# Second product of the second feed-forward: 512-wide accumulation replaced by seven 256-wide Strassen products for three of four block pairs

## Chip, cores and metric

The kernel runs on one core of a Trainium2 chip. The metric is device microseconds of one execution. The engines are called as in the profile: PE (TensorE matmuls), PEld (its weight loads), DVE (VectorE), ACT (ScalarE), POOL (GpSimd) and SP (the queue that issues almost all DMAs). A difference of less than 0.2% (3 us) can hardly be told from no change here.

## What is computed

A cross attention of 8 batches (512 tokens and 32 states each, 8 heads of 64) gives 4352 rows of 512 values: 8 blocks of 512 tokens and one block of 256 state rows. They pass through two feed-forward layers; the second one is what the change touches:

```python
def _moe_ref(x, w_gate, w_val, w_out) -> np.ndarray:
    gate = 1.0 / (1.0 + np.exp(-(x @ w_gate)))
    val = x @ w_val
    return (gate * val @ w_out).astype(np.float32)

def _moe2_ref(x, w_in, w_out) -> np.ndarray:
    h = x @ w_in
    r = np.maximum(h, 0.0)
    g = r * r
    return (g @ w_out).astype(np.float32)
```

`w_in` is 512 x 2048 and `w_out` 2048 x 512. All matmuls take every operand as a high and a low part (`h`, `l`), so one product of two tiles is three matmuls (`mm3`, lines 182 to 184 before).

## The kernel before

The program has a first part (attention, weight conversion, first feed-forward, up to about 795 us) and a second part, the second feed-forward. Python code emits instructions; a scheduler then sets each engine's order, so that work of neighbouring steps is interleaved on PE. The second part goes over the 8 token blocks in `NP` = 4 pairs `p`. A pair has `NQ` = 8 steps `q`, each for 256 of the 2048 hidden columns.

`front(p, q)` forms the hidden values of both blocks by Strassen's method: seven products P1 to P7 of sums of x blocks (made once for each pair by `x_steps`, split into `xh`, `xl` by `split_x`) with sums of `w_in` blocks (`wi`, made in the first part). A product is 6 matmuls of 512 columns, so a front has 42. The PSUM tiles are `px`, `py`, `pz`; ACT copies intermediate sums out (`snap`), DVE joins them (`joined`), and `squared` applies relu and square and splits the result `c` into `g2h`, `g2l`.

`back(p, b, r, nt)` is the second product, called after q = 2, 4, 6, 7 with r = 0 to 3: for one block `b` and four 128-row pieces of `w_out` (`wo[f]`) it accumulates, for each 128-token tile, 12 matmuls of 512 columns into a PSUM tile `o`; the result goes to `y2` by an ACT copy (r = 0) or a DVE add (r > 0), and out by DMA after r = 3. `load_wo(r)` loads four `wo` tiles of 512 KB. At the end of a pair, with `apart`, the matmuls on the older pieces come first and `x_steps(p + 1)` is emitted around `back`.

In pair 0, `load_late` and `convert_late` still convert the second half of `w_out` and store it in DRAM; POOL's only work in the second part is their subtraction `ul` (line 661). In the last pair the 256 state rows go along: `state_front` (24 matmuls of 256 columns for each q, PSUM tile `pst`) and `back(p, 2, ...)`.

Of the kernel before, what the change touches and what calls it, by code (L numbers as in the profile page):

```python
# [8 lines left out]
F32 = mybir.dt.float32  # L9
# [9 lines left out]
P = 128  # L19
# [13 lines left out]
def kernel(  # L33
# [127 lines left out]
    def width(b):  # L161
        return S if b < B else NSTATE
# [13 lines left out]
    NQ = NF2 // 2  # L176
    wi_dram = {q: dram.tile([P, 8, 2, 256], F32, name=f"wi{q}") for q in range(NQ)}
    wo_dram = {f: dram.tile([P, 2, 512], F32, name=f"wo{f}") for f in range(NF2)}
    y_dram = {b: dram.tile([P, KD, width(b)], F32, name=f"yd{b}") for b in blocks}

    def mm3(ps, lh, ll, rh, rl, start, stop, more=False):
# [550 lines left out]

    def close_one():
        one.close()
        for name, bufs in (("wo", 4), ("g2", 24), ("y2", 8), ("t2", 1)):
# [27 lines left out]
        wi_done[1] += 1  # L763
        return wi.pop(key)

    def load_wo(r):
        for f in range(4 * r, 4 * r + 4):
            t = two["wo"].tile([P, 2, 512], F32R, tag="wo", name="wo")
            nc.sync.dma_start(out=t.bitcast(F32), in_=wo_dram[f])
            wo[f] = t  # L770

    def load_xin(p, i):
        half, b = ((0, 0), (0, 1), (1, 1), (1, 0))[i]
# [11 lines left out]
    def x_steps(p):  # L785

        t1, t2 = {}, {}

        def one_two(k):
            b11, b12, b22 = (xin[p, i, j][:, k, :] for i, j in ((0, 0), (0, 1), (1, 1)))  # L790
            split_x(p, "P1", k, b11)
            t1[k] = cv_p.tile([P, S], F32, tag="c", name="t1")
            nc.vector.tensor_sub(out=t1[k], in0=b12, in1=b11)
            split_x(p, "P5", k, t1[k])
            t2[k] = q_p.tile([P, S], F32, tag="q", name="t2")
            nc.vector.tensor_sub(out=t2[k], in0=b22, in1=t1.pop(k))
# [27 lines left out]
    def snap(ps, name):  # L824
        t = two["t2"].tile([P, S], F32, tag=name, name=name)
        nc.scalar.copy(out=t, in_=ps)  # L826
        return t
# [14 lines left out]
        nc.vector.tensor_sub(out=l, in0=c, in1=h.bitcast(F32))  # L842
        g2[key] = (h, l)

    def front(p, q):
# [16 lines left out]
        squared((p, 0, 2 * q), joined(y, p1))
        product(x, p, q, "P7", False)
        c22 = joined(x, p5)
        product(z, p, q, "P3", False)
        squared((p, 1, 2 * q + 1), c22)
        product(x, p, q, "P4", False)
        squared((p, 1, 2 * q), joined(z, u))
        squared((p, 0, 2 * q + 1), x, raw=True)

    def back(p, b, r, nt, apart=False):
        fs = range(4 * r, 4 * r + 4)
        accs2 = [acc_p.tile([P, S], F32, tag=f"acc{t}", name=f"o{t}") for t in range(nt)]
        order = [(t, f) for t in range(nt) for f in fs]
        if apart:
            order.sort(key=lambda k: k[1] // 2)
        for t, f in order:
            ts = slice(t * P, (t + 1) * P)
            gh, gl = g2[p, b, f]
            mm3(  # L880
                accs2[t], gh[:, ts], gl[:, ts], wo[f][:, 0, :], wo[f][:, 1, :],
                f == fs[0], f == fs[-1],
            )
            if f < fs[-1]:
                continue
            acc = accs2[t]
            if r == 0:
                y = (two["y2"] if b < 2 else yo_p).tile([P, DM], F32, tag="y2" if b < 2 else "y", name="y2")
                y2[b, t] = y
                nc.scalar.copy(out=y, in_=acc)  # L890
                continue
            y = y2[b, t]
            nc.vector.tensor_add(out=y, in0=acc, in1=y)  # L893
            if r < NQ // 2 - 1:
                continue
            if b == 2:
                for i in range(4):
                    r0 = (4 * t + i) * (S + NS) + S
                    (nc.scalar if i % 2 else nc.sync).dma_start(
                        out=out[r0 : r0 + NS, :], in_=y[NS * i : NS * (i + 1), :]  # L900
                    )
            else:
                r0 = (2 * p + b) * (S + NS) + t * P
                nc.sync.dma_start(out=out[r0 : r0 + P, :], in_=y)

    def prep_state_x():
        t = two["t2"].tile([P, KD, NSTATE], F32, tag="xst", name="xst")
        nc.sync.dma_start(out=t, in_=y_dram[B])
        for k in range(2):
            h = gs_p.tile([P, 2, NSTATE], F32R, tag="gh", name="sth")  # L910
            l = gs_p.tile([P, 2, NSTATE], F32R, tag="gl", name="stl")
# [3 lines left out]
            xop["s", k] = (h, l)  # L915

    def state_front(p, q):
# [10 lines left out]
        hl = raw_p.tile([P, 2, 2 * NSTATE], F32R, tag="raw", name="g2s")  # L928
        squared("s", ps.rearrange("p i n -> p (i n)"), raw=True, into=(hl[:, 0], hl[:, 1]))
        h, l = g2.pop("s")  # L930
        for i in range(2):
            cols = slice(i * NSTATE, (i + 1) * NSTATE)
            g2[p, 2, 2 * q + i] = (h[:, cols], l[:, cols])

    HALF = NF1 // 2
    segments = [(b, 0, HALF) for b in range(QB)] + [(b, HALF, NF1) for b in range(QB)]
# [105 lines left out]

    step = lambda: None
    close_one()
    load_wo(0)
    for fn in x_steps(0):
        fn()
    last = NP - 1
    for p in range(NP):
        for q in range(NQ):  # L1050
            if p == 0 and q > 2:
                convert_late()
            if p == 0 and q == 2:
                load_late(EARLY)
            front(p, q)
            if p == last and q == 0:
                prep_state_x()
            if p == last:
                state_front(p, q)
            if p < last and NQ - 5 < q < NQ - 1:  # L1060
                load_xin(p + 1, q - NQ + 4)
            if q < 2 or q % 2 and q < NQ - 1:
                continue
            steps = []
            if q == NQ - 1:
                steps = x_steps(p + 1) if p < last else []
                for fn in steps[:3]:
                    fn()
            r = (q - 1) // 2
            for b in range(2):  # L1070
                back(p, b, r, NT, apart=q == NQ - 1)
                if p == 0:
                    convert_late()
                for fn in [] if b else steps[3:]:
                    fn()
            if p == last:
                back(p, 2, r, NSTATE // P)
            if (p, r) != (last, NQ // 2 - 1):
                load_wo((r + 1) % (NQ // 2))


# [28 lines left out]
```

## Time and profile before

| | us |
|---|---|
| median of 3 runs (1497.92 to 1499.72) | 1499.65 |
| the profiled execution, its own time | 1500.54 |
| its span, first to last instruction | 1498.8 |
| PE busy in the span | 1431.0 (95%) |
| DVE busy | 940.2 (63%) |
| ACT busy | 748.8 (50%) |
| POOL busy | 246.0 (16%) |

The profile is of one execution; 1.7 us of its own time lie outside the span. A matmul's busy time is longer than its share of the engine, since matmuls are pipelined: how fast PE works is read from the distance between the starts of neighbouring matmuls. Some matmul records are missing from the trace.

### The profile page before, as it was taken

To read this page: it belongs to the slowest core of one execution; us is meant where nothing else is said; L and a number is where in the kernel's file an instruction comes from. 1 tells how busy PE (TensorE), PEld (TensorE's weight loads), DVE (VectorE), ACT (ScalarE), POOL (GpSimd) and SP (SyncE) were. 2 spreads that over 40 slices of the span, in tenths; PEclk is the share of its full clock that TensorE was granted. 3 is DMA by queue.
4 is the path that set the end of the run, shared out by engine and by line. 5 is a ranking of instruction groups with operands and counts; after the bars stand their busy time and mean duration, and the time that the engine had idled before them with its cause. 6 is when DMAs were issued, how large, how long until landed. Compare 5 with 4: busy or idle time off the path is not lost.

```text
span 1498.8 us, 19379 instructions
## 1 busy us (share of the span) xinstructions
PE 1431.0 (95%) x6552; PEld 1176.9 (79%) x6552; DVE 940.2 (63%) x1579; ACT 748.8 (50%) x1291; POOL 246.0 (16%) x216
## 2 busy tenths in 40 slices
PE   5879999999999989999899999999999999999998
PEld 3558878887787677888798788888888888888887
DVE  7986887578889987555536655734575356433443
ACT  6865876456678887666424522332242223232211
POOL 1112213232344544333101100000000000000000
PEclk9889999999999999999999999999999999999999
DMA  9984799699999864333677844644365443645442
GB/s 265 341 263 120 229 328 339 210 363 292 323 296 286 254 211 145 95 113 92 242 271 250 274 158 147 217 146 143 133 227 188 151 152 134 222 124 195 155 145 80
DMA packets 244595, 311.68 MB, mean 208 GB/s; under 512 B 105361, under 2 KB 152977, under 8 KB 244497
## 3 DMA queue, kind: packets, MB, share of 16 engines
q1 hardware_dynamic: 242224, 309.66, 63.8%
q10 hardware_dynamic: 2272, 0.79, 0.3%
q8 instruction: 52, 0.85, 0.2%
q14 instruction: 47, 0.38, 0.1%
HBM read 221.25 MB, written 89.13 MB: 207 GB/s over the span
## 4 chain that ended last, share of the span: by engine, by line
PE 72%; DVE 10%; ACT 7%; DMA 7%; issue 3%; SPq 1%; POOL 0%; ACTq 0%; DVEq 0%; POOLq 0%
PE o L182 8%; PE o L183 8%; PE o L184 8%; PE px L183 4%; PE px L182 4%; PE px L184 4%; PE acc L183 4%; PE acc L184 3%; PE acc L182 3%; DMA raw<-in_moe_w_out_dram 2%; PE psg L182 2%; PE psg L183 2%; PE psg L184 2%; PE psv L182 2%; PE psv L183 2%
## 5 line engine op out<-in xcount | busy, mean ns | idle before, releaser
L182 PE MATMUL o<-wo,g2h 128*128 128x512 f32 x512 | 198.6, 390 | 3.7 <-DMA wo<-wo 3.0
L183 PE MATMUL o<-wo,g2h 128*128 128x512 f32 x512 | 199.1, 389 | 0.0
L184 PE MATMUL o<-wo,g2l 128*128 128x512 f32 x512 | 193.9, 389 | 0.0
L537 POOL TENSOR_TENSOR gg<-gi,gg 128x512 fp32r<-128x512 f32 x96 | 135.3, 1412 | 350.5 <-ACT gg L536 284.2
L183 PE MATMUL acc<-gl,o 128*128 128x512 f32 (+1 forms) x432 | 164.4, 381 | 3.7 <-DVE gl L190 3.7
L184 PE MATMUL acc<-gh,o 128*128 128x512 f32 (+1 forms) x432 | 163.0, 378 | 0.0
L841 ACT CAST g2h<-c 128x512 fp32r<-128x512 f32 x96 | 59.3, 622 | 178.8 <-DVE c L837 178.8
L182 PE MATMUL acc<-gh,o 128*128 128x512 f32 (+1 forms) x432 | 139.3, 380 | 0.6 <-DVE y L624 0.4
L893 DVE TENSOR_TENSOR y<-o,y 128x512 f32<-128x512 f32 x102 | 68.5, 688 | 103.5 <-PE o L184 102.8
L182 PEld LDWEIGHTS o<-wo,g2h 128*128 128x128 f32 x512 | 96.1, 188 | 24.9 <-ACT p L826 3.0
L184 PEld LDWEIGHTS o<-wo,g2l 128*128 128x128 f32 x512 | 96.1, 188 | 19.8
L183 PEld LDWEIGHTS o<-wo,g2h 128*128 128x128 f32 x512 | 96.2, 188 | 19.5
L190 DVE TENSOR_TENSOR gl<-g,gh 128x512 fp32r<-128x512 f32 (+1 forms) x108 | 88.4, 818 | 36.3 <-ACT gh L189 35.8
L182 PE MATMUL px<-xh,wi 128*128 128x512 f32 x256 | 99.8, 390 | 0.0
L183 PE MATMUL px<-xl,wi 128*128 128x512 f32 x256 | 99.7, 389 | 0.0
L184 PE MATMUL px<-xh,wi 128*128 128x512 f32 x256 | 99.6, 389 | 0.0
L183 PEld LDWEIGHTS acc<-gl,o 128*128 128x128 f32 x432 | 81.3, 188 | 21.3 <-DVE gl L190 6.9
L182 PEld LDWEIGHTS acc<-gh,o 128*128 128x128 f32 x432 | 80.6, 189 | 17.4 <-DVE y L624 1.1
L184 PEld LDWEIGHTS acc<-gh,o 128*128 128x128 f32 x432 | 81.3, 188 | 14.6
L182 PE MATMUL psg<-a,gg 128*128 128x512 f32 x192 | 78.6, 409 | 14.8 <-ACT sg L550 12.1
L556 DVE TENSOR_TENSOR g<-psv,sg 128x512 f32<-128x512 f32 x96 | 65.6, 683 | 35.4 <-PE psv L184 21.6
L189 ACT CAST gh<-g 128x512 fp32r<-128x512 f32 (+1 forms) x108 | 64.3, 596 | 40.4 <-DVE g L556 23.0
(188 smaller groups left out, 3268.7 us busy)
## 6 DMA issues: line engine op xcount, KB each, us to landing
wi<-wi SPq DMA_DIRECT2D x256, 256.0 KB, 3.1
wo<-wo SPq DMA_DIRECT2D x64, 512.0 KB, 5.5
gd<-go SPq DMA_DIRECT2D x192, 128.0 KB, 4.4
gi<-gd SPq DMA_DIRECT2D x96, 256.0 KB, 4.0
wi<-wa SPq DMA_DIRECT2D x32, 512.0 KB, 5.0
wd<-w SPq DMA_DIRECT2D x24, 512.0 KB, 5.1
ws<-wd SPq DMA_DIRECT2D x24, 512.0 KB, 6.7
raw<-in_moe_w_out_dram SPq DMA_DIRECT2D x20, 512.0 KB, 6.2
```

The source lines that it names most:

```text
L182: nc.tensor.matmul(ps, lh, rh, start=start, stop=False, skip_group_check=more)
L183: nc.tensor.matmul(ps, lh, rl, start=False, stop=False, skip_group_check=more)
L184: nc.tensor.matmul(ps, ll, rh, start=False, stop=stop, skip_group_check=more)
L189: nc.scalar.copy(out=gh[:, :n], in_=g32[:, :n])
L190: nc.vector.tensor_sub(out=gl[:, :n], in0=g32[:, :n], in1=gh[:, :n].bitcast(F32))
L537: nc.gpsimd.tensor_sub(out=t[:, 1], in0=src, in1=t[:, 0].bitcast(F32))
L556: nc.vector.tensor_mul(out=g32, in0=ps, in1=sg)
L841: nc.scalar.copy(out=h, in_=c)
L893: nc.vector.tensor_add(out=y, in0=acc, in1=y)
```

## The change

For pairs 1 to 3 the second product also goes by Strassen's method. The hidden values of a pair for one q are four 512-token blocks `c` (block b, hidden half i). `g_steps` makes sums of them on POOL (`s1`, `s2` and one in place), and splits all seven operands on ACT and DVE into `gh`, `gl`. `back_pairs` runs seven products for each r: a product has 24 matmuls of 256 columns (8 output tiles of 128 tokens by 256 columns, two q, three each), 168 for each r, where the two calls of `back` had 96 of 512 columns. Its weights are halves of `wo`, or sums of `w_out` blocks, that lie in DRAM as `wt`; a tile `wp` is two DMAs of 256 KB, four tiles ahead (`feed_wo`). The PSUM tiles are of 2 x 256 columns; after every product both are added to, or copied to, a half of `y2`: 14 evacuations for each r, where there were 8.

The weight sums are made in pair 0: `add_wo` (POOL, for each q two adds of 512 columns and four of 256) and `split_wo` (ACT cast, DVE subtraction, four DMAs of 256 KB). Pair 0's own second product stays as it was. `x_steps` emits the operands product by product and takes its subtractions to POOL for pairs 2 and 3. In the last pair `state_back(q)` does the state rows for each q, with as many matmuls as before. The core of the diff:

```diff
+    BACK = [
+        ("P1", "x", 0, 0), ("P5", "z", 1, 1), ("P6", "x", 0, 1), ("P3", "z", 0, 1),
+        ("P7", "x", 1, 1), ("P2", "y", 0, 0), ("P4", "x", 1, 0),
+    ]
...
+    def feed_wo():
+        while wo_done[0] < min(wo_done[1] + 4, len(wo_plan)):
...
+            else:
+                t = two["wo"].tile([P, 2, 2, 256], F32R, tag="wo", name="wp")
+                p, r, k = key
+                for i in range(2):
+                    q = 2 * r + i
+                    n, e = (PLAIN if k in PLAIN else SUMS)[k]
+                    w = wo_dram[2 * q + n] if k in PLAIN else wt_dram[q][:, :, n, :]
+                    nc.sync.dma_start(
+                        out=t[:, i].bitcast(F32), in_=w[:, :, 256 * e : 256 * (e + 1)]
+                    )
...
+    def add_wo(q):
+        c = []
+        for f in (2 * q, 2 * q + 1):
+            t = gs_p.tile([P, 2, 256], F32, tag="gh", name="wc")
+            w = wo[0, f].bitcast(F32)
+            nc.gpsimd.tensor_add(
+                out=t.rearrange("p e x -> p (e x)"), in0=w[:, 0, :], in1=w[:, 1, :]
+            )
+            c.append(t)
+        b1, b2 = c
+        nc.gpsimd.tensor_sub(out=b1[:, 0], in0=b1[:, 1], in1=b1[:, 0])
+        nc.gpsimd.tensor_sub(out=b1[:, 1], in0=b2[:, 1], in1=b1[:, 1])
+        nc.gpsimd.tensor_sub(out=b2[:, 1], in0=b2[:, 1], in1=b1[:, 0])
+        nc.gpsimd.tensor_sub(out=b2[:, 0], in0=b2[:, 0], in1=b2[:, 1])
+        sums[q] = c
...
+        sub = (nc.gpsimd if p > 1 else nc.vector).tensor_sub
...
+    def g_steps(p, q):
+
+        def split(name, src):
+            pool, tag = (yo_p, "y") if name == "P4" else (two["g2"], "g2")
+            h, l = [pool.tile([P, S], F32R, tag=tag, name=n) for n in ("gh", "gl")]
+            nc.scalar.copy(out=h, in_=src)
+            nc.vector.tensor_sub(out=l, in0=src, in1=h.bitcast(F32))
+            gop[p, q, name] = (h, l)
...
+        def p1():
+            v["s1"] = cv_p.tile([P, S], F32, tag="c", name="s1")
+            nc.gpsimd.tensor_add(out=v["s1"], in0=c(1, 0), in1=c(1, 1))
+            split("P1", c(0, 0))
+
+        def p5():
+            v["s2"] = q_p.tile([P, S], F32, tag="q", name="s2")
+            nc.gpsimd.tensor_sub(out=v["s2"], in0=v["s1"], in1=c(0, 0))
+            split("P5", v["s1"])
...
+    def back_pairs(p, r, extra, apart=False, between=None):
...
+            for j, t, k in order:
+                h, l = gop[p, 2 * r + k, name]
+                ts = slice((2 * j + t) * P, (2 * j + t + 1) * P)
+                mm3(
+                    ps[to, j][:, t], h[:, ts], l[:, ts], w[:, k, 0], w[:, k, 1],
+                    start and t == k == 0, k == 1, not (start and t == 0),
+                )
+            drop_wo((p, r, name))
+            for j in range(2):
...
+                y = y2[b, j][:, :, 256 * e : 256 * (e + 1)]
+                if r == 0 and name in ("P1", "P5", "P6", "P4"):
+                    nc.scalar.copy(out=y, in_=ps[to, j])
+                else:
+                    nc.vector.tensor_add(out=y, in0=ps[to, j], in1=y)
...
+            if q == NQ - 1:
+                rest_of(extra)
+                steps = x_steps(p + 1) if p < last else []
+                between = (lambda: state_back(NQ - 1)) if p == last else None
+                back_pairs(p, NR - 1, steps, apart=True, between=between)
+                rest_of(steps)
+            elif q and q % 2 == 0:
+                back_pairs(p, q // 2 - 1, extra)
+                rest_of(extra)
```

The order of instructions up to the end of the first part stays as it was. Three places show what moves after it.

DVE at the end of a pair, before (pair 1 to pair 2): four evacuations `y`, then the low parts `xl` of the next pair's operands and the subtractions `t` that two of them need.

```order
L893 TENSOR_TENSOR y_10140<-o_10746,y_10140 128x512 [waits PE_49]
L893 TENSOR_TENSOR y_10154<-o_10747,y_10154 128x512 [waits PE_49]
L893 TENSOR_TENSOR y_10168<-o_10748,y_10168 128x512 [waits PE_49]
L893 TENSOR_TENSOR y_10182<-o_10749,y_10182 128x512 [waits PE_49]
L782 TENSOR_TENSOR xl<-xin,xh 128x512 [waits PE_49,Activation_49]
L782 TENSOR_TENSOR xl<-t_10907,xh 128x512 [waits PE_49,Activation_49]
L803 TENSOR_TENSOR t_11001<-xin 128x512 [waits DVE_49]
L782 TENSOR_TENSOR xl<-t_10913,xh 128x512 [waits PE_49,Activation_49]
```

DVE at the same place now: evacuations alternate with `gl` (operands of this pair's second product) and `xl` (of the next pair's first).

```order
L1051 TENSOR_TENSOR y_10281<-o,y_10281 128x2x256 [waits PE_49]
L1051 TENSOR_TENSOR y_10283<-o,y_10283 128x2x256 [waits PE_49]
L852 TENSOR_TENSOR xl<-t,xh 128x512 [waits Activation_49]
L991 TENSOR_TENSOR gl<-s_11450,gh 128x512 [waits Activation_49]
L991 TENSOR_TENSOR gl<-c,gh 128x512 [waits Activation_49] x2
L1051 TENSOR_TENSOR y_10281<-o,y_10281 128x2x256 [waits DVE_49,PE_49]
L1051 TENSOR_TENSOR y_10283<-o,y_10283 128x2x256 [waits DVE_49,PE_49]
L852 TENSOR_TENSOR xl<-t,xh 128x512 [waits Activation_49]
L1051 TENSOR_TENSOR y_10320<-o,y_10320 128x2x256 [waits PE_49]
L852 TENSOR_TENSOR xl<-xin,xh 128x512 [waits DMAHW3_49,Activation_49]
```

From the first of the 14 evacuations of this r to the join of the next front's `px` there are 36 instructions on DVE: 14 evacuations and 2 joins (one input in PSUM) and 20 others (two inputs in SBUF).

PE, first front of the next pair, before: product P7 into `px` waits for its weights and for ACT, for no low part from DVE, and tiles `o` stand around it.

```order
L182 MATMUL px<-xh,wi 128x512 [waits DMAHW1_49,Activation_49]
L183 MATMUL px<-xl,wi 128x512
L184 MATMUL px<-xh,wi 128x512
```

PE at the same place now: P2, P7 and P3 follow one another, and each low part `xl` is waited for by itself.

```order
L184 MATMUL py<-xl,wi 128x512 [waits DVE_49]
L185 MATMUL py<-xh,wi 128x512
L183 MATMUL px<-xh,wi 128x512 [waits DMAHW2_49,Activation_49]
L184 MATMUL px<-xl,wi 128x512 [waits DVE_49]
L185 MATMUL px<-xh,wi 128x512
L183 MATMUL px<-xh,wi 128x512
L184 MATMUL px<-xl,wi 128x512 [waits DVE_49]
L185 MATMUL px<-xh,wi 128x512
L183 MATMUL pz<-xh,wi 128x512 [waits DMAHW3_49]
L184 MATMUL pz<-xl,wi 128x512 [waits DVE_49]
```

POOL, which ended before with eight `ul` of pair 0, now has, at the end of pair 1, the sums `s` and the in-place sum `c` of the last q among the subtractions `t` of `x_steps(2)`.

```order
L1001 TENSOR_TENSOR s_11444<-c 128x512
L865 TENSOR_TENSOR t<-xin 128x512
L1006 TENSOR_TENSOR s_11450<-s_11444,c 128x512
L1010 TENSOR_TENSOR c<-c 128x512
L865 TENSOR_TENSOR t<-xin,t 128x512
L865 TENSOR_TENSOR t<-xin 128x512
L1014 TENSOR_TENSOR s_11450<-c,s_11450 128x512
L865 TENSOR_TENSOR t<-xin 128x512
```

Twelve POOL instructions stand in this chain, and ACT casts and DVE's `gl` and `xl` wait for them one by one.

## Rows read from the trace of the kernel before

**Rows 1.** Windows, the four pairs: window, length, busy (count) by engine, PEclk, DMA share, GB/s

```profile
797.00:957.00 160.00, 156.96 (x696) 129.36 (x695) 104.63 (x166) 65.08 (x114) 11.46 (x8) 1.00 0.63 218
957.00:1120.00 163.00, 163.00 (x721) 134.97 (x720) 86.29 (x135) 50.03 (x86) 0.00 (x0) 1.00 0.50 168
1120.00:1284.00 164.00, 164.00 (x732) 136.06 (x732) 86.67 (x135) 49.55 (x85) 0.00 (x0) 1.00 0.47 161
1284.00:1495.00 211.00, 210.04 (x1006) 176.14 (x1004) 87.29 (x135) 50.06 (x86) 0.00 (x0) 1.00 0.45 152
```

**Rows 2.** Waits of PE, 797 to 1499 us: us in total, times, longest

```profile
PE o L182 <- DMA wo<-wo: 3.0, 2, 2.6
PE o L182 <- ACT g2h L841: 0.5, 1, 0.5
```

**Rows 3.** Timeline of PE: the first and last of 21 matmuls of 512 columns

```profile
1483.64 0.39 PE L182 MATMUL o<-wo,g2h 128*128 128x512 f32 x1
...
1488.17 0.39 PE L184 MATMUL o<-wo,g2l 128*128 128x512 f32 x1
```

**Rows 4.** Timeline of PE: the first and last of 52 matmuls of 256 columns

```profile
769.83 0.28 PE L183 MATMUL acc<-gl,o 128*128 128x256 f32 x1
...
775.95 0.28 PE L183 MATMUL psg<-sp,ws 128*128 128x256 f32 x1
```

**Rows 5.** Groups of DVE, 957 to 1284 us: busy, mean ns, idle before

```profile
L893 DVE TENSOR_TENSOR y<-o,y 128x512 f32<-128x512 f32 x52 | 34.5, 687 | 48.0 <-PE o L184 47.9
L842 DVE TENSOR_TENSOR g2l<-c,g2h 128x512 fp32r<-128x512 f32 x48 | 32.6, 688 | 11.7 <-ACT g2h L841 10.8
```

**Rows 6.** Groups of ACT, 957 to 1284 us

```profile
L841 ACT CAST g2h<-c 128x512 fp32r<-128x512 f32 x48 | 29.8, 622 | 78.7 <-DVE c L837 78.7
```

**Rows 7.** Groups of DVE, 300 to 600 us

```profile
L190 DVE TENSOR_TENSOR gl<-g,gh 128x512 fp32r<-128x512 f32 x42 | 36.3, 864 | 9.8 <-ACT gh L189 9.6
L556 DVE TENSOR_TENSOR g<-psv,sg 128x512 f32<-128x512 f32 x42 | 28.6, 680 | 7.8 <-ACT sg L550 6.4 <-PE psv L184 1.0
```

**Rows 8.** Groups of POOL, 300 to 600 us

```profile
L537 POOL TENSOR_TENSOR gg<-gi,gg 128x512 fp32r<-128x512 f32 x42 | 62.5, 1490 | 123.3 <-ACT gg L536 91.0 <-issue 22.5 <-DMA gd<-go 4.1
L690 POOL TENSOR_TENSOR c<-c 128x256 f32<-128x256 f32 x7 | 6.4, 912 | 11.4 <-DVE wa L698 8.3 <-DVE xs_t L428 3.1
```

**Rows 9.** Windows of the first part, columns as in Rows 1

```profile
300.00:400.00 100.00, 96.81 (x423) 78.58 (x422) 80.45 (x126) 62.33 (x102) 31.59 (x29) 1.00 0.98 331
400.00:500.00 100.00, 96.42 (x431) 77.73 (x430) 87.91 (x153) 81.58 (x136) 48.42 (x43) 0.98 0.96 286
500.00:600.00 100.00, 89.85 (x392) 69.76 (x392) 81.42 (x147) 80.26 (x137) 44.21 (x35) 0.98 0.64 197
600.00:700.00 100.00, 100.00 (x479) 83.68 (x478) 56.56 (x107) 67.01 (x118) 37.20 (x29) 1.00 0.36 99
```

**Rows 10.** Waits of PE, 300 to 600 us

```profile
PE psg L182 <- ACT sg L550: 7.5, 9, 3.0
PE acc L183 <- DVE gl L190: 3.5, 5, 1.6
PE psv L182 <- DVE g L556: 1.5, 5, 0.4
PE ps_so L420 <- DVE sw L411: 1.4, 1, 1.4
...
PE ps_s L183 <- DVE xtl L308: 0.8, 1, 0.8
```

**Rows 11.** Windows within pair 0, columns as in Rows 1

```profile
797.00:820.00 23.00, 22.59 (x105) 18.39 (x104) 18.73 (x30) 12.95 (x23) 2.78 (x2) 1.00 0.97 341
840.00:860.00 20.00, 17.37 (x77) 14.08 (x76) 12.81 (x20) 9.86 (x17) 4.63 (x4) 1.00 0.97 346
```

**Rows 12.** DMA issues, 797 to 1499 us: count, KB each, median us to landing

```profile
wi<-wi SPq DMA_DIRECT2D x245, 256.0 KB, 3.1
wo<-wo SPq DMA_DIRECT2D x64, 512.0 KB, 5.5
```

More of the change, by code (lines that the diff above doesn't have):

```diff
@@ L178 @@
     wo_dram = {f: dram.tile([P, 2, 512], F32, name=f"wo{f}") for f in range(NF2)}
+    wt_dram = {q: dram.tile([P, 2, 2, 512], F32, name=f"wt{q}") for q in range(NQ)}
     y_dram = {b: dram.tile([P, KD, width(b)], F32, name=f"yd{b}") for b in blocks}
@@ L764, in take_wi @@
         return wi.pop(key)
[L766 to L770, printed above, removed]
+    BACK = [
+        ("P1", "x", 0, 0), ("P5", "z", 1, 1), ("P6", "x", 0, 1), ("P3", "z", 0, 1),
+        ("P7", "x", 1, 1), ("P2", "y", 0, 0), ("P4", "x", 1, 0),
+    ]
+    NR = NQ // 2
+    wo_plan = [(0, f) for f in range(NF2)]
+    for p in range(1, NP):
+        for r in range(NR):
+            own = [(p, r, k) for k, _, _, _ in BACK]
+            if p < NP - 1:
+                wo_plan += own
+                continue
+            side = [(p, f) for f in range(4 * r, 4 * r + 4)]
+            if r < NR - 1:
+                wo_plan += side + own
+            else:
+                wo_plan += side[:2] + own[:3] + side[2:] + own[3:]
@@ new lines, in split_wo @@
+    def split_wo(q):
+        for i, c in enumerate(sums.pop(q)):
+            c = c.rearrange("p e x -> p (e x)")
+            h = gs_p.tile([P, 512], F32R, tag="gl", name="th")
+            nc.scalar.copy(out=h, in_=c)
+            nc.sync.dma_start(out=wt_dram[q][:, 0, i, :], in_=h.bitcast(F32))
+            l = gs_p.tile([P, 512], F32R, tag="gl", name="tl")
+            nc.vector.tensor_sub(out=l, in0=c, in1=h.bitcast(F32))
+            nc.sync.dma_start(out=wt_dram[q][:, 1, i, :], in_=l.bitcast(F32))
@@ L872, in back @@
+    def back(b, r, apart=False):
         fs = range(4 * r, 4 * r + 4)
[L873 to L874 removed]
+        accs2 = [acc_p.tile([P, S], F32, tag=f"acc{t}", name=f"o{t}") for t in range(NT)]
+        order = [(t, f) for t in range(NT) for f in fs]
         if apart:
@@ L1044 @@
     close_one()
-    load_wo(0)
-    for fn in x_steps(0):
-        fn()
+    feed_wo()
     last = NP - 1
-    for p in range(NP):
-        for q in range(NQ):
[L1051 to L1057, printed above, removed]
+    rest_of(x_steps(0))
+    for q in range(NQ):
+        if q > 2:
+            convert_late()
+        if q == 2:
+            load_late(EARLY)
+        front(0, q, [])
+        if NQ - 5 < q < NQ - 1:
+            load_xin(1, q - NQ + 4)
+        if q < 2 or q % 2 and q < NQ - 1:
+            continue
+        r = (q - 1) // 2
+        steps = x_steps(1) if q == NQ - 1 else []
+        for fn in steps[:7]:
+            fn()
+        add_wo(2 * r)
+        back(0, r, apart=q == NQ - 1)
+        convert_late()
+        rest_of(steps[7:])
+        split_wo(2 * r)
+        add_wo(2 * r + 1)
+        back(1, r, apart=q == NQ - 1)
+        convert_late()
+        split_wo(2 * r + 1)
+        drop_wo(*[(0, f) for f in range(4 * r, 4 * r + 4)])
+    y2.clear()
+    for p in range(1, NP):
+        extra = []
+        for q in range(NQ):
+            front(p, q, extra)
+            extra = g_steps(p, q)
             if p == last:
+                if q == 0:
+                    prep_state_x()
+                else:
+                    state_back(q - 1)
                 state_front(p, q)
```

231 lines of the change are left out of this document (161 added, 70 removed).

## Prediction

> **What bounds the kernel now.** I first read the windows over the four pairs [rows 1], the second column being PE's busy time: PE is busy for nearly the whole length of each (163.00 of 163.00, 164.00 of 164.00), at a granted clock of 1.00 (2.4 GHz). DVE is busy for about 53% of the two middle pairs, ACT for 31%, POOL not at all. Then the waits of PE over the second part: 3.5 us in 702, of which 3.0 are for `wo` [rows 2]. So the second part is PE's issue of matmuls and nothing else, and its length is a count of matmuls times the distance between two starts. For 512 columns that distance is (1488.17 - 1483.64) / 20 = 0.2265 us [rows 3]. For 256 columns, with another weight tile for each matmul, it is (775.95 - 769.83) / 51 = 0.1200 us [rows 4], not half but 53%. The check: 8 fronts of 42 and 4 backs of 96 are 336 + 384 = 720 matmuls, times 0.2265 is 163.1 us, which is the length of a middle pair.
>
> **Matmuls removed and added.** A pair's second product was 384 x 0.2265 = 87.0 us. By Strassen's method it is 4 x 168 = 672 matmuls of 256 columns, 672 x 0.1200 = 80.6 us: seven eighths of the columns, but more starts, so 7.3% is saved and not 12.5%. That is 6.34 us for a pair, 156.7 instead of 163.1, and 19.0 us for pairs 1 to 3. The state rows keep their matmuls. Everything else is a question of whether PE still never waits.
>
> **DVE in pairs 1 and 2.** A pair now has 174 DVE instructions of 128 x 512 values: 72 with an input in PSUM (24 joins, 48 additions to `y2`) and 102 with both inputs in SBUF (24 squares, 8 products of relu, 56 `gl`, 14 `xl`). Without work on POOL either kind takes 0.688 us [rows 5] (I take the 2 x 256 shape of the new evacuations as 512 columns), so 119.7 us, 76% of 156.7. ACT casts about 110 tiles at 0.62 us [rows 6], 44%: free. But POOL now works in these pairs, and between 300 and 600 us, where it works too, a DVE instruction with two SBUF inputs took 864 ns, one from PSUM 680 [rows 7]. POOL's 32 sums and 8 subtractions are 40 x 1.490 [rows 8] = 59.6 us, 38% of the pair; in that stretch it was busy for 31.59 + 48.42 + 44.21 us [rows 9], 41%, so its price is the nearest. With it, 72 x 0.688 + 102 x 0.864 = 137.6 us, 88%. That is below the length of the pair, so DVE doesn't become the bound; this needs a mean of (156.7 - 49.5) / 102 = 1.05 us, above any of these rows.
>
> A busy share of 88% without a wait isn't likely, though. The nearest stretch is the same 300 to 600 us, with DVE at 80 to 88% and POOL at 32 to 48%, where PE was busy for 90 to 97% [rows 9]. PE's waits on DVE there were 3.5 + 1.5 + 1.4 + 0.8 = 7.2 us [rows 10], 2.4% (the 7.5 us for `sg` are an ACT result that the second part doesn't have). At 600 to 700 us, with DVE at 57%, there was none [rows 9]. I take 2.4% of 2 x 156.7 us, that is 7.5 us; the ends are 0 and twice that.
>
> Where they would lie: the PSUM pair of a product must be evacuated (2 x 0.688 us) before the product two later needs it, while a product gives PE 24 x 0.120 = 2.88 us, so DVE keeps up with about two splits for each product. The tight place is the end of a pair, where the last sums of `g`, the subtractions of the next pair's x and the 14 evacuations meet. From the first of these evacuations to the join of the next `px` DVE has 36 instructions, 16 x 0.688 + 20 x 0.864 = 28.3 us, and PE has about 28.8 us of work in the same stretch (seven products of 2.88 and six groups of six matmuls, 36 x 0.2265, with 0.5 to spare). So about 3 us of waits at each of these two places is already within the 7.5. Behind a late `gl` on DVE stands the next evacuation, and behind that the next product on PE.
>
> **Pair 3.** 192 DVE instructions (86 from PSUM) at the same prices are 86 x 0.688 + 106 x 0.864 = 150.8 us in about 201 us, 75%, with state matmuls to fill in; no next pair follows. Between 0 and 2.4% of 201, that is 0 and 4.8: I take 1.5. The last work is now the state rows of the last step, after the evacuation of the last product: 0.3 us.
>
> **Pair 0.** `add_wo` gives POOL 16 additions of 512 columns and 32 of 256, 16 x 1.490 + 32 x 0.912 [rows 8] = 53.0 us; `split_wo` gives DVE 16 subtractions, which add at least 16 x 0.864 = 13.8 us to its 104.6 [rows 1], 74%, and at most, with every instruction dearer by 0.864 / 0.688, come to 145 us, 91%. The 32 writes of 256 KB are 8.4 MB, 52 GB/s over 160 us on top of 218 [rows 1]. The mean has room, but at 797 to 820 and 840 to 860 us the DMA engines were already at a share of 0.97, with 341 and 346 GB/s [rows 11], and PE waited 3.0 us for `wo` there [rows 2]. Below, the cost is 0 (the writes fall later, and are needed only in pair 1); above, it is the same wait twice more, 6 us. I take 3.
>
> **Weights.** The reads for a second product grow from 16 x 512 KB = 8.4 MB to 56 x 256 KB = 14.7 MB a pair, 40 GB/s more over 157 us on 161 to 168 [rows 1], far below the 331 of [rows 9]. A tile is asked for four tiles ahead, 3 products or 8.6 us before its need at the least, and a transfer of 256 KB lands after 3.1 us, one of 512 KB after 5.5 [rows 12]. Hidden; if not, PE waits some 0.5 to 2 us at each r.
>
> **Sum.** -19.0 + 7.5 + 1.5 + 3.0 + 0.3 = -6.7 us. From the profiled execution's 1500.5 that is 1493.8; this execution lies 0.9 above the median of 1499.65, so 1493 us for the median. 0.2%, 3 us, is what can be told from no change here.
>
> **The rivals.**
>
> *The waits are hidden (0.20).* PE always has matmuls of a front or of another product ahead of those that wait, as at 600 to 700 us, and the pairs come out at 157 us. The sums of 0 to 5 us of waits give 1481 to 1486 us. For it speaks that the products of the second matrix are mixed with those of the next front; against it that DVE's share is 88% and not 57%.
>
> *The waits eat the gain (0.16).* With twice the rate, 4.8% in pairs 1 and 2 and 2.4% in pair 3, plus 6 us in pair 0: -19.0 + 15.0 + 4.8 + 6.0 + 0.3 = +7.1 at the extreme, and about 0 with two of these three. 1497 to 1503 us.
>
> *DVE becomes the bound through POOL (0.14), slower.* Its place is pairs 1 and 2, in the two-input splits `gl`, `g2l` and `xl`, beside POOL's `s` and `t`. The price of sharing that the rows show is 864 - 680 or 688 ns, at 41% POOL [rows 7, 9]. It decides from a mean of 1.05 us on; where DVE needs (163.8 - 49.5) / 102 = 1.12 us, a pair is 163.8 us long and, with the other terms as above, nothing is left of the gain. Each further 0.1 us costs 20 us in two pairs, so 1503 to 1521 us for 1.15 to 1.24 us. If DVE stood still for the whole of each POOL instruction, a pair would need 119.7 + 59.6 = 179.3 us, 22.6 above PE's, 45 in two pairs: -19.0 + 45.2 + 4.8 gives about 1531 us, the far end. Against it: between 300 and 600 us DVE and POOL were busy for 249.8 and 124.2 us of 300 [rows 9], and the dearer instruction grew by 26% only.
>
> The Trainium skill speaks for this rival: "SBUF — State Buffer", section "Who interferes with whom", says that a DVE instruction with two SBUF inputs and a GpSimd instruction that reads SBUF shut each other out for a whole instruction, and that one with at most one SBUF input is free of it. The trace agrees on who is hit (864 against 680 ns), and shows less than a whole POOL instruction as the mean price. By the rule at its hardest the time would be the 1531 just worked out.
>
> **How the numbers follow.** The forecast, 1493 us with 1487 to 1499 of its own (waits of 7 to 19 us in all), has 0.50. The range is 1482 to 1504: it leaves out the best of the hidden case and most of the last one, some 0.2. Faster by more than 3 us (below 1496.6): all of the hidden case, 0.44 of the forecast's 0.50, and a little of the third, 0.66. Within 3 us: the rest of the forecast's and most of the third, 0.19. Slower: 0.15.
>
> **What would show it.** The matmuls of 256 columns into `o` start 0.120 us apart, and the windows of pairs 1 and 2 are 157 us plus their waits. In the groups of DVE, `gl` and `xl` take 0.8 to 0.9 us and `y` 0.68; a mean of `gl` above 1.05 shows the last rival. PE's waits name DVE (`y` or `gl`) and lie at the pair ends, 2 to 5 us each; POOL is busy for about 60 us in each of pairs 1 and 2 and 65 in pair 0. In pair 0 PE's waits are for `wo` or `wi` and total under 9 us.
>
> **What would make it wrong.** A pitch above 0.120 us when three operands stream in (at 0.130 the gain falls from 19.0 to (87.0 - 87.4) x 3, to nothing); a POOL chain of sums that is late for its product, since twelve POOL instructions, 17.9 us, stand before the last of them at a pair's end; or an evacuation held up behind a split that waits for ACT.

## The result and the profile after

The changed kernel takes 1507.17 us (median of 6 runs, 1505.35 to 1513.54) against 1499.49 us before: a ratio of 1.0061, 95% interval 1.0041 to 1.0081. It is slower; 1493 was forecast, with a range up to 1504. Run again beside other kernels it gave 1.0048 (1.0035 to 1.0062). Its profiled execution took 1510.27 us, its span 1508.5.

The windows of the four pairs, which answer to [rows 1]: window, length, busy (count) of PE, PEld, DVE, ACT and POOL, PEclk, DMA share, GB/s.

```profile
797.00:963.00 166.00, 160.71 (x710) 131.21 (x709) 129.92 (x178) 72.58 (x131) 70.67 (x56) 1.00 0.76 260
963.00:1122.00 159.00, 157.50 (x968) 140.93 (x967) 120.40 (x162) 56.75 (x101) 55.08 (x36) 1.00 0.61 197
1122.00:1285.00 163.00, 158.39 (x1007) 142.70 (x1005) 129.43 (x174) 61.88 (x110) 62.93 (x40) 1.00 0.62 203
1285.00:1504.00 219.00, 211.63 (x1359) 191.29 (x1357) 158.87 (x213) 69.16 (x125) 55.30 (x36) 1.00 0.69 225
```

POOL's 55 to 63 us in the middle pairs are near the forecast's 59.6, DVE's 120 to 129 below its 137.6. New is that PE is no longer busy for the whole length of the two middle pairs. The longest of its waits over the second part, against the two of [rows 2]: us in total, times, longest.

```profile
PE o L183 <- DMA wp<-wt: 3.9, 3, 3.4
PE px L183 <- DVE c L936: 2.2, 3, 1.1
PE pz L184 <- DVE xl L852: 1.9, 1, 1.9
PE pst L184 <- DVE sthl L1133: 1.7, 1, 1.7
PE pz L183 <- ACT p L905: 1.5, 1, 1.5
PE pz L183 <- DVE c L936: 1.4, 2, 0.7
PE o L183 <- DVE y L1051: 1.2, 3, 0.5
```

This view counts idle time after a matmul's modelled end, which is later than the time at which the next could have started. Below, a wait is measured by starts: the distance from one matmul to the next, less 0.1200 us (256 columns) or 0.2265 us (512 columns), where more than 0.15 us is left. So counted, PE waits 23.4 us in the second part, 4.3 before. The second part is taken from the first `px` matmul to the start of the last matmul of all: 792.75 to 1494.30 before, 701.5 us; 797.35 to 1503.87 now, 706.5 us. The change costs 5.0 us there, where the sum had -6.7. The first part, whose order of instructions is unchanged, ended 4.6 us later in this execution.

DVE and POOL in the second part, as groups (busy, mean ns), to set beside [rows 5, 7, 8]; the POOL rows are of pairs 1 and 2:

```profile
L1051 DVE TENSOR_TENSOR y<-o,y 128x512 f32<-128x512 f32 x144 | 95.7, 682 | 30.3 <-PE o L185 30.1
L991 DVE TENSOR_TENSOR gl<-c,gh 128x512 fp32r<-128x512 f32 x96 | 81.9, 863 | 18.9 <-ACT gh L990 18.4
L991 DVE TENSOR_TENSOR gl<-s,gh 128x512 fp32r<-128x512 f32 x72 | 64.5, 899 | 18.7 <-ACT gh L990 17.4
L852 DVE TENSOR_TENSOR xl<-t,xh 128x512 fp32r<-128x512 f32 x24 | 23.9, 1003 | 2.2 <-ACT xh L851 2.1
...
L1010 POOL TENSOR_TENSOR c<-c 128x512 f32<-128x512 f32 x16 | 28.0, 1748 | 0.0
L1001 POOL TENSOR_TENSOR s<-c 128x512 f32<-128x512 f32 x16 | 24.4, 1528 | 175.2 <-DVE c L980 168.6 <-ACT gh L990 6.7
```

The means are almost those that the forecast took, 682 and 863 ns against 0.688 and 0.864; only `xl` after a subtraction, 1003 ns, lies above the 0.8 to 0.9 us named for it. The mean hides what happens to single instructions, at the end of a pair above all. DVE, POOL and PE there, between pairs 2 and 3 (start, us, engine, line, what):

```profile
1274.19 1.57 DVE L991 TENSOR_TENSOR gl<-s,gh 128x512 fp32r<-128x512 f32 x1
1275.68 1.77 DVE L977 TENSOR_TENSOR c<-c 128x512 f32<-128x512 f32 x1
1277.37 1.75 DVE L852 TENSOR_TENSOR xl<-t,xh 128x512 fp32r<-128x512 f32 x1
...
1282.32 1.29 DVE L1051 TENSOR_TENSOR y<-o,y 128x512 f32<-128x512 f32 x2 [1.41 <-PE o L185]
...
1273.46 1.75 POOL L865 TENSOR_TENSOR t<-xin 128x512 f32<-128x512 f32 x1
1275.17 1.73 POOL L1006 TENSOR_TENSOR s<-s,c 128x512 f32<-128x512 f32 x1
1276.87 1.70 POOL L1010 TENSOR_TENSOR c<-c 128x512 f32<-128x512 f32 x1
1278.53 1.74 POOL L865 TENSOR_TENSOR t<-xin,t 128x512 f32<-128x512 f32 x1
...
1282.04 1.28 POOL L1014 TENSOR_TENSOR s<-c,s 128x512 f32<-128x512 f32 x1
...
1276.87 0.39 PE L183 MATMUL pz<-xh,wi 128*128 128x512 f32 x1
1279.17 0.50 PE L184 MATMUL pz<-xl,wi 128*128 128x512 f32 x1 [1.91 <-DVE xl L852]
```

From 1273.46 on POOL runs instruction after instruction of 1.7 us, and the three DVE instructions with two SBUF inputs beside them take 1.6 to 1.8 us, not 0.69: the two engines go in step, one DVE instruction for each of POOL's. Both pay: beside the two `y`, which have an input in PSUM, POOL's instruction takes 1.28 us. The `xl` that PE wants is the third in such a row, and PE waits 2.1 us for it. In the second part 105 of the 690 tensor operations on DVE took 1.1 us or more; before it was 3 of 538.

### The profile page after: what moved, and what is told of

Read it like the earlier page. It is cut to its first block, busy times and chain, and to the rows that moved or that the text cites. A ratio compares the mean times of both kernels' runs of the same rounds, so it can differ in the third digit from the quotient of the medians.

```text
span 1508.5 us, 21836 instructions
## 1 busy us (share of the span) xinstructions
PE 1422.5 (94%) x7416; PEld 1202.4 (80%) x7416; DVE 1111.4 (74%) x1731; ACT 790.8 (52%) x1379; POOL 477.6 (32%) x376
## 4 chain that ended last, share of the span: by engine, by line
PE 53%; DVE 18%; DMA 14%; ACT 8%; issue 5%; POOL 2%; SPq 1%; ACTq 0%; DVEq 0%; POOLq 0%
PE o L183 6%; PE o L185 5%; PE o L184 5%; PE acc L184 3%; PE acc L185 3%; PE acc L183 3%; PE px L183 3%; PE px L184 3%; PE px L185 3%; DVE gl L991 2%; PE psg L183 2%; PE psv L183 2%; PE psv L185 2%; PE psv L184 2%; PE psg L184 2%
## 5 line engine op out<-in xcount | busy, mean ns | idle before, releaser
L183 PE MATMUL o<-wp,gh 128*128 128x256 f32 x672 | 189.5, 284 | 5.8 <-DMA wp<-wt 3.9
L184 PE MATMUL o<-wp,gh 128*128 128x256 f32 x672 | 188.8, 283 | 0.0
L185 PE MATMUL o<-wp,gl 128*128 128x256 f32 x672 | 185.8, 284 | 0.1
L183 PEld LDWEIGHTS o<-wp,gh 128*128 128x128 f32 x672 | 128.5, 191 | 10.3 <-issue 4.4
L184 PEld LDWEIGHTS o<-wp,gh 128*128 128x128 f32 x672 | 128.5, 191 | 2.2
L1001 POOL TENSOR_TENSOR s<-c 128x512 f32<-128x512 f32 x24 | 36.9, 1538 | 288.8 <-DVE c L980 274.8
L185 PEld LDWEIGHTS o<-wp,gl 128*128 128x128 f32 x672 | 126.6, 191 | 1.5 <-DVE gl L991 0.7
L1051 DVE TENSOR_TENSOR y<-o,y 128x512 f32<-128x512 f32 x144 | 95.7, 682 | 30.3 <-PE o L185 30.1
L990 ACT CAST gh<-s 128x512 fp32r<-128x512 f32 x72 | 44.7, 621 | 109.3 <-POOL s L1014 76.5
L990 ACT CAST gh<-c 128x512 fp32r<-128x512 f32 x96 | 56.7, 619 | 79.9 <-PE o L184 41.9
L991 DVE TENSOR_TENSOR gl<-c,gh 128x512 fp32r<-128x512 f32 x96 | 81.9, 863 | 18.9 <-ACT gh L990 18.4
L183 PEld LDWEIGHTS acc<-gh,o 128*128 128x128 f32 x432 | 80.8, 189 | 18.0 <-ACT gh L190 1.2
```

The lines of the kernel that those rows point to most:

```text
L183: nc.tensor.matmul(ps, lh, rh, start=start, stop=False, skip_group_check=more)
L184: nc.tensor.matmul(ps, lh, rl, start=False, stop=False, skip_group_check=more)
L185: nc.tensor.matmul(ps, ll, rh, start=False, stop=stop, skip_group_check=more)
L1001: nc.gpsimd.tensor_add(out=v["s1"], in0=c(1, 0), in1=c(1, 1))
L1051: nc.vector.tensor_add(out=y, in0=ps[to, j], in1=y)
```

## The experiments

In the table, "second part" and "waits" are measured as above, in one profiled execution each; "first ends" is the first `px` matmul. Some traces have stretches of the second part in which PE is granted half its clock (last section); 512-column matmuls count there as waits of 0.2 us each, which is 2.2 us of the 29.8 in e7_unused and 1.6 of the 14.0 in e9_x_pool.

| kernel | ratio to before | interval | second part | waits | first ends |
|---|---|---|---|---|---|
| before | 1 | | 701.5 | 4.3 | 792.7 |
| changed | 1.0061 | 1.0041 to 1.0081 | 706.5 | 23.4 | 797.4 |
| changed, again | 1.0048 | 1.0035 to 1.0062 | 710.8 | 25.9 | 793.4 |
| e1_tail | 1.0039 | 1.0023 to 1.0054 | 702.7 | 18.3 | 792.6 |
| e2_no_sums | 0.9978 | 0.9966 to 0.9990 | 693.7 | 12.4 | 799.3 |
| e3_wt_copy | 1.0020 | 1.0012 to 1.0029 | 700.5 | 18.4 | 794.8 |
| e4_sums_dve | 1.0010 | 0.9999 to 1.0021 | 700.6 | 18.8 | 794.9 |
| e5_dram | 1.0003 | 0.9990 to 1.0015 | 701.4 | 4.2 | 794.7 |
| e6_all | 0.9955 | 0.9941 to 0.9969 | 691.9 | 11.1 | 795.4 |
| e7_unused | 1.0093 | 1.0073 to 1.0112 | 715.3 | 29.8 | 795.2 |
| e8_wt_dve | 1.0027 | 1.0013 to 1.0040 | 705.0 | 19.4 | 793.5 |
| e9_x_pool | 0.9949 | 0.9931 to 0.9967 | 694.8 | 14.0 | 797.5 |
| e10_g_pool | 0.9991 | 0.9982 to 1.0001 | 698.1 | 15.9 | 796.5 |
| e11_square | 0.9945 | 0.9929 to 0.9962 | 691.1 | 10.8 | 794.7 |

My theory after the result: POOL's instructions stand in DVE's way, and in the way of ACT's casts in their chain; the last weight tiles come late; the first part has nothing to do with it. The rivals: DVE simply has too many instructions; the transfers collide; or the first part was lengthened by the change.

**e1_tail, the last weight tiles.**

```diff
-                wo_plan += side[:2] + own[:3] + side[2:] + own[3:]
+                wo_plan += side[:2] + own[:3] + side[2:] + own[3:5]
...
+        for k in ("P2", "P4"):
+            ts = [two["x"].tile([P, 2, 256], F32R, tag="x", name="wx") for _ in range(2)]
```

> The weights of the last two products of the last r of pair 3 are loaded early into four tiles of the x pool instead of the wo pool; nothing is left out. Theory A (the last products have only one product of lead, because state tiles hold two of the four wo buffers, so a weight tile comes 3.6 us late behind the output stores): the waits for wp after 1480 us fall from 4.5 us to under 1.5, and the kernel is 3 to 4 us faster than the changed kernel (about 1503.5 us by its median). Rival B (the transfers at the end are limited by the DMA engines, whatever their order): the same wait shows up at another tile or in the outputs, and the time stays within 1 us of 1507.

In the changed kernel the chain of work that ended last shows the transfer (start, us, what), and PE's timeline the wait:

```profile
1491.26 6.68 DMA wp<-wt
...
1498.08 0.36 PE L183 MATMUL o<-wp,gh 128*128 128x256 f32 x1 [3.40 <-DMA wp<-wt]
```

The tile of the last product is issued one product ahead and lands after 6.68 us; the median of the `wp` tiles from `wt` is 3.5. Two of the four `wo` buffers are held by the state rows' tiles of the last step, whose matmuls come last of all. With the early load the waits for `wp` fall to 0.6 us in the whole second part, and the second part by 3.8 us, although this trace has 1.7 us of loss to half clock that the changed kernel's hasn't. The ratio falls by 0.0022 (3.3 us) against the first measurement of the changed kernel and by 0.0009 (1.4 us) against the second. Theory A holds for the waits; that the time falls is likely, but the intervals overlap.

**e2_no_sums and e7_unused: no work on POOL in pairs 1 to 3, and the same work with no operand waiting for it.** The second differs from the first by POOL's lines alone:

```diff
+            v["s2"] = q_p.tile([P, S], F32, tag="q", name="s2")
+            nc.gpsimd.tensor_sub(out=v["s2"], in0=v["s1"], in1=c(0, 0))
             split("P5", c(1, 1))
...
+            sub(out=t, in0=a, in1=b)
             return a if p > 1 else t
```

> Leaves out the sums and differences on POOL in pairs 1 to 3 (of hidden values and, for pairs 2 and 3, of x): the operands are plain blocks, so POOL is idle after pair 0, while the DVE, ACT and PE instructions of a pair stay as many. Theory A (POOL's sharing with DVE and its chain into the splits make the waits of the pairs): gl falls from 863 to about 690 ns, the waits of PE between 970 and 1480 us fall from 13 us to under 4, and the time is 8 to 10 us below the changed kernel's, about 1498 us. Rival B (DVE's own number of instructions makes them): gl gets faster all the same, but the waits stay above 8 us and less than 4 us are gained.

> Leaves out the use of the sums made in pairs 1 to 3: POOL makes all 32 or 40 of a pair as before, but the operands are plain blocks, so nothing waits for POOL and DVE only shares with it. Theory A (the sharing itself makes most of the waits): gl stays at 830 ns or more, the waits between 970 and 1480 us stay above 8 us, and the time is above 1503 us. Rival B (the chain from POOL through ACT's casts to DVE makes them): gl stays slow all the same, but the waits fall below 5 us and the time to 1497 us, near that without the sums (1495.6).

The groups of `gl` in pairs 1 and 2, first without the sums:

```profile
L993 DVE TENSOR_TENSOR gl<-c,gh 128x512 fp32r<-128x512 f32 x113 | 75.2, 687 | 19.7 <-ACT gh L992 18.9
```

and with sums that nothing uses:

```profile
L991 DVE TENSOR_TENSOR gl<-c,gh 128x512 fp32r<-128x512 f32 x112 | 114.6, 1044 | 19.0 <-ACT gh L990 17.8
```

Without POOL the second part is 12.8 us shorter than the changed kernel's. With POOL at work and no operand waiting for it, it is 8.8 us longer than the changed kernel's and 21.6 longer than without (some 5 us of it in two stretches at half clock, last section), and `gl` has a mean of 1.04 us. So POOL's work beside DVE costs the time: theory A holds, and the chain of waits through POOL into the operands isn't needed for it. Not all of the 21.6 us need be DVE's: 7.3 us of PE's waits are for `wi`, and SP's queue still stands twice for 1.0 us until POOL has read an `xin` tile. How much comes by that way wasn't tested. That e7_unused is even worse than the changed kernel fits POOL's instructions now running whenever they can, but I didn't test it apart.

**e4_sums_dve, e10_g_pool and e9_x_pool: who makes the sums.** `e4_sums_dve` is the changed kernel with

```diff
-            nc.gpsimd.tensor_sub(out=v["s2"], in0=v["s1"], in1=c(0, 0))
+            nc.vector.tensor_sub(out=v["s2"], in0=v["s1"], in1=c(0, 0))
...
-        sub = (nc.gpsimd if p > 1 else nc.vector).tensor_sub
+        sub = nc.vector.tensor_sub
```

and so for all sums of `g_steps`; the other two put back one or the other in e6_all (below).

> Nothing is left out: the sums of hidden values and of x in pairs 1 to 3 are made by DVE instead of POOL. DVE then has 214 instructions in a pair, about 147 us of 157 at 0.688. Theory A (number of DVE instructions is what binds once POOL is gone): the waits of PE in pairs 1 and 2 rise from 8 us to 12 or more and the time is 2 to 8 us above the changed kernel's, about 1512 us. Rival B (sharing with POOL and its slow chain are dearer than 0.69 us on DVE): the waits fall below 6 us and the time is 2 to 5 us below, about 1503 us.

> As e6_all, but the 32 sums of hidden values of a pair go back to POOL (x and the weight sums stay on DVE); nothing is left out. Theory A: it is these that make most of the sharing, so gl takes above 800 ns, the waits between pairs rise from 3.3 us to 4 to 5 and the time is 3 to 5 us above e6_all, near 1498.5. Rival B (the subtractions of x at the pair's end are what costs): within 1 us of e6_all.

> As e6_all, but the 8 subtractions of x in each of pairs 2 and 3 go back to POOL; nothing is left out. Theory A (a POOL instruction beside DVE costs more than the 0.69 us that it saves there, most of all at a pair's end): the waits between pairs rise from 3.3 us each to 4 or more and the time is 1 to 3 us above e6_all. Rival B (at a pair's end it is DVE's count that binds): they fall below 2 us each and the time is 2 to 3 us below e6_all.

Here my theory A for e4_sums_dve fell: with 40 more instructions on DVE in pairs 1 and 2 the second part is 5.9 us shorter than the changed kernel's. PE's waits in these two pairs fall from 8.2 to 2.7 us, and the ones that remain name `wi`, not DVE. So 0.69 us on DVE is cheaper than POOL's instruction beside it. With the 32 sums back on POOL (e10_g_pool) PE's waits in pairs 1 and 2 are 8.4 us, 7.3 of them for DVE; e6_all has 3.3 there, all for `wi`. The second part is 6.2 us longer than e6_all's, 1.7 us of it in a stretch at half clock (last section), and the ratio 0.0036 higher, a little more than expected. With only the 8 subtractions of x back (e9_x_pool) the second part is 2.9 us longer in the trace, but the ratio isn't; 1.7 us of it is a stretch at half clock. That run decides nothing.

**e3_wt_copy and e8_wt_dve: pair 0.** The first stores plain weights in place of the sums; the second is

```diff
-            nc.gpsimd.tensor_add(
+            nc.vector.tensor_add(
```

and so for the five other lines of `add_wo`.

> Leaves out the making of the weight sums in pair 0 (POOL's additions, ACT's casts and DVE's subtractions): the 32 writes of 256 KB stay, but copy the plain weights. Theory A (pair 0 waits on DVE, which has these subtractions and POOL beside it): the waits in pair 0 fall from 6.3 us to the 3.4 us of before, and the time is about 3 us below the changed kernel's, 1504 us. Rival B (the writes collide with the reads): the waits of pair 0 stay above 5.5 us and the time is within 1 us of 1507.

> Nothing is left out: only the additions for the weight sums in pair 0 are moved from POOL to DVE. Theory A (pair 0 waits because of POOL: single DVE instructions of 1.7 us beside it, and ACT standing still for up to 7 us before a cast of POOL's result): the waits of pair 0 fall from 6.3 us to under 3 and the time to 1503 us. Rival B (DVE is full in the first half of pair 0, so 23 us more on it are dearer): the waits of pair 0 rise above 7 us and the time to 1509 us.

PE's waits in pair 0, 6.3 us in the changed kernel, are 0.5 us with the plain copies, more than the 3 us that I had expected to get back, since the waits for `wo` of before (all of its 3.4 us) are gone too. The longer one, 2.8 us, isn't gone by an earlier load: counted from the first `px`, the `wo` tile is asked for at 51.0 us before and in e3_wt_copy and at 51.5 in the changed kernel, and lands at 56.6 in all three. What differs is PE's order: between the last matmul of the first r and the first of the second it had 13 matmuls of a front before, and has 23 in the changed kernel and 30 in e3_wt_copy. So the 32 writes cost nothing that can be seen; making the sums costs 5.8 us. With the additions on DVE 2.1 us are left. At the end of pair 0 ACT shows how POOL got in the way there: it stands with a cast of a weight sum at the head of its queue, ahead of the copy `p` of `pz` for which PE then waits 1.5 us (us in total, times, longest; 940 to 965 us).

```profile
ACT th L836 <- POOL wc L827: 9.8, 2, 7.0
```

**e5_dram and the changed kernel again: the first part.**

```diff
+    wt_dram = {q: dram.tile([P, 2, 2, 512], F32, name=f"wt{q}") for q in range(NQ)}
     y_dram = {b: dram.tile([P, KD, width(b)], F32, name=f"yd{b}") for b in blocks}
```

> The kernel before, with the 8 MB of the changed kernel's weight sums declared in DRAM and not used, so that what is declared behind them lies elsewhere; no instruction differs. Theory A (the first part's end, 792.7 us in the trace of before and 792.6 to 799.3 us in those of the changed kernel and its variants, varies with the clock of the first 110 us and not with the change): the time is that of before, 1498.5 us within 1. Rival B (the place of the DRAM tensors slows the first part): 1501 to 1503 us.

> The changed kernel as it is, with a second trace. Theory A (of its 7.7 us, 5.0 are the second part, the same in each execution, and the rest is the first part's own variation): the second part takes 706.5 us within 0.5 again, the first ends between 791 and 796 us, and the time is 5 to 6 us above that of before. Rival B (the change lengthens the first part by 3 us or more, though its instructions stand in the same order): the first part ends after 796 us again and the time is 8 us or more above.

The tensors alone change nothing. In the second trace of the changed kernel the first part ended at 793.4 us, and over all traces between 792.6 and 799.3, with no order to it: theory A in that, though with two traces of the unchanged program a lengthening by 1 or 2 us can't be ruled out. But the second part took 710.8 us and not 706.5, so it isn't the same in each execution, as I had written; 2.5 us of that are waits, and 1.7 us come from 3.4 us at half clock behind the last wait for `wp`.

**e6_all and e11_square: what beats both.** e6_all is e1_tail, e4_sums_dve and e8_wt_dve together; e11_square moves one square of each front to ACT:

```diff
-            nc.vector.tensor_mul(out=r, in0=r, in1=r)
+            nc.scalar.activation(out=r, in_=r, func=AF.Square)
```

> The changed kernel with nothing left out and POOL without any part in the change: the sums of hidden values, of x and, in pair 0, of weights are made by DVE, and the last two weight tiles are loaded early, as in e1_tail. Theory A (sharing with POOL, ACT's wait for it and the late tiles cost 13 to 16 us together): the second part takes 692 us (before 701.5, changed 706.5), its waits fall below 11 us, and the time is 1492 us, below before. Rival B (DVE, with 214 instructions a pair and 48 more in pair 0, becomes late itself): pair 0 waits more than 8 us and the time is no less than 1498.

> As e6_all, but one square of each front in pairs 1 to 3 is made by ACT instead of DVE, 8 DVE instructions less in a pair. Theory A (what is left of the waits is DVE's count): the second part gets 1 to 2 us shorter than 691.9 us. Rival B (what is left is order, at the pair's end and the state rows): it stays within 0.5 us, or gets longer by the longer chain on ACT.

e6_all: 1494.27 us, a ratio of 0.9955 (0.9941 to 0.9969), faster than both kernels. Its second part takes 691.9 us, 9.6 less than before. Windows of its pairs 1 and 2, and its longest waits:

```profile
961.00:1121.00 160.00, 159.14 (x1007) 144.21 (x1007) 129.28 (x207) 58.82 (x104) 0.00 (x0) 1.00 0.64 200
1121.00:1277.00 156.00, 153.82 (x981) 139.80 (x980) 130.71 (x210) 60.00 (x108) 0.00 (x0) 1.00 0.66 209
...
PE px L183 <- DMA wi<-wi: 2.8, 4, 0.9
PE pst L183 <- DMA wi<-wi: 1.7, 1, 1.7
PE pz L183 <- DMA wi<-wi: 1.1, 3, 0.6
```

DVE is busier than in the changed kernel (81 to 84%) and PE waits half as long, now mostly for `wi`; waits for DVE have all but gone (0.4 us in this view). Eight DVE instructions less in a pair (e11_square) shorten the second part by 0.8 us, between the two expectations, and the ratio can't be told from e6_all's: inconclusive. Why `wi` comes late in e6_all wasn't tried.

## Why the prediction was wrong

- **What bounds the kernel, and the matmuls removed and added: right.** The part is PE's issue, and the 256-column matmuls do start 0.120 us apart. 1152 matmuls of 512 columns less and 2016 of 256 more save 19.0 us, if nothing else changes.
- **DVE in pairs 1 and 2: right in sum, wrong in what was behind it.** Forecast 7.5 us of waits, measured 8.2 (1.3 within the pairs, 4.2 and 2.7 at their ends, where the prediction had about 3 each); 1.1 of them are for a `wi` tile and about 6 for DVE. Even the busy time at the end holds: the 36 instructions between pairs 1 and 2 were to take 28.3 us, and DVE was busy for 28.3. But that is partly luck, for no instruction there has the price that I took. POOL is busy for 41% between 300 and 600 us and for 70% from 1268 to 1288:

```profile
1268.00:1288.00 20.00, 17.78 (x117) 15.73 (x117) 16.55 (x19) 6.86 (x12) 13.96 (x9) 1.00 0.51 163
```

Of the 20 instructions with two SBUF inputs at the end of pair 1, 12 took 0.68 us and the other 8 between 1.1 and 1.8 us; the mean of all 20 is 1.0 us. The groups from 1107.4 to 1137.9 us:

```profile
L1051 DVE TENSOR_TENSOR y<-o,y 128x512 f32<-128x512 f32 x14 | 9.2, 677 | 0.0
L852 DVE TENSOR_TENSOR xl<-t,xh 128x512 fp32r<-128x512 f32 x8 | 7.6, 954 | 1.8 <-ACT xh L851 1.8
L991 DVE TENSOR_TENSOR gl<-c,gh 128x512 fp32r<-128x512 f32 x3 | 3.6, 1228 | 0.1
```

So the sum went by a mean, and what PE waits for is a single late instruction, the `xl` of 1277.37 above. I excluded the price of a whole POOL instruction because the mean was only 26% dearer. It is paid, but by some instructions and not over the length of the pairs: the mean of `gl` never reached the last rival's 1.05 us. What the Trainium skill's "SBUF — State Buffer", section "Who interferes with whom", says (one of the two stands for a whole instruction) is nearly what the single instructions show: one of each, 0.69 and 1.28 us when undisturbed, takes 1.7 us in step, where one after the other would be 1.97. I had held the mean against it.
- **Weights: wrong, and with it pair 3.** "Four tiles ahead, 3 products or 8.6 us" fails in the last r, where two of the four buffers belong to the state rows. Its end has 4.9 us of waits, where before had 1.0, and pair 3 another 4.0; forecast were 1.5 and 0.3 for all of it. Of these 8.9 us 6.4 are for weight tiles (`wp` 5.3, `wi` 1.1), and 1.9 for the low part of the state rows on DVE (`sthl`). In e1_tail the last r waits 0.9 us.
- **Pair 0: right in size for the wrong reason.** Forecast 3 us more, measured 2.9; but 5.8 us are the making of the sums, and 2.9 were given back since PE no longer waits for `wo`. I had put it on DMA first; e3_wt_copy shows that the writes are free.
- **A term that was missing: 4.9 us.** The sum took one distance between starts for each width. Matmuls that wait for nothing come more slowly. The first one after most of the 28 waits is about 0.11 us late on top of the wait (0.50 us busy, not 0.39, in the `pz` row above), and many 512-column matmuls among 256-column ones start 0.2317 us apart and not 0.2267, as the `px` here against the `pz`, six each:

```profile
1100.63 0.40 PE L183 MATMUL px<-xh,wi 128*128 128x512 f32 x1
...
1102.02 0.39 PE L183 MATMUL pz<-xh,wi 128*128 128x512 f32 x1
...
1103.38 0.28 PE L183 MATMUL o<-wp,gh 128*128 128x256 f32 x1
```

By the starts, the first kind makes 2.4 of the 4.9 us, the second kind together with waits under 0.15 us the rest. Why these matmuls come more slowly isn't shown.

Together: -19.0 + 8.2 + (4.0 + 4.9 - 1.0) + 2.9 + 4.9 = +4.9 us, against +5.0 measured. So two steps of the forecast's -6.7 failed: the weight tiles that were "hidden" (pair 3 with its end is off by 6.1 us, mostly for them) and the constant distance between starts (4.9). The rest is off by 0.7. The medians differ by 7.7 us. What is above the 5.0 lies partly in stretches at half clock behind waits, which the first trace doesn't have within the part and the second has; how much of it is the first part's variation stays open.

Of the other rivals, "the waits eat the gain" (1497 to 1503) named the right cause for its sum but was 4 us short of the time. The last rival's own range is added up wrongly: by its prices 1.15 to 1.24 us give 1506 to 1524, not 1503 to 1521. And PE's work at a pair's end, seven products and 36 matmuls, is 28.3 us, not 28.8, so there was nothing to spare. With POOL left out and the last two weight tiles loaded early, e6_all is at 1494.27, 6 us below before in the same session, about the gain that was forecast; with POOL left out of pairs 1 to 3 alone, e4_sums_dve has no gain (1.0010).

## What to carry to other kernels

A mean duration beside a busy neighbour is a mixture: it can give the sum of a stretch and still hide how late one instruction comes, so look at single instructions in the stretch where another engine waits. Work that is moved to an idle engine isn't free if it slows the engine that was to be relieved; here 40 sums a pair were cheaper on the DVE that was thought to be full. A look-ahead of so many buffers is worth only what other users of the same buffers leave, so follow it to the last tile.

## What was not expected of the hardware

Two engines in step: DVE's two-input instruction and POOL's, back to back, take 1.7 us each at a pair's end; a DVE instruction with an input in PSUM stays at 0.68, and POOL's beside it at 1.28. And a wait of PE can cost twice: in e9_x_pool the granted clock falls from 1.00 to 0.50 (2.4 to 1.2 GHz) for 3.4 us right after PE had waited for `wi`, and the same matmuls then start 0.43 us apart. Windows around it, columns as above:

```profile
1137.00:1140.50 3.50, 1.60 (x9) 1.07 (x8) 3.41 (x6) 0.80 (x3) 0.00 (x0) 1.00 1.02 382
1140.50:1143.90 3.40, 3.40 (x10) 2.64 (x9) 1.29 (x2) 1.52 (x3) 0.00 (x0) 0.50 0.60 211
1143.90:1147.00 3.10, 3.10 (x15) 2.55 (x14) 2.68 (x5) 1.10 (x2) 0.00 (x0) 1.00 0.39 114
...
1139.68 0.49 PE L183 MATMUL px<-xh,wi 128*128 128x512 f32 x1 [1.73 <-DMA wi<-wi]
```

This stretch costs 1.7 us. The kernel before and e6_all have none within the second part; the second trace of the changed kernel, e1_tail, e7_unused, e8_wt_dve and e10_g_pool have one or two, of 3.4 us, or 6.8 at the end of e7_unused. Each begins during a wait of PE of 1.9 us or more, or within 1.3 us after it, at a pair's end or at the last wait for `wp`. But not every such wait is followed by one: in the first trace of the changed kernel the clock stays at 1.00 behind waits of 2.1 and 3.6 us.
